# Hash attention and two MLPs on one core: two PSUM side jobs a pair put into one step, integer weight work moved, start copies and a scaling reissued

## The chip, the core and the metric

The kernel runs on one core of a Trainium2 chip. TensorE multiplies matrices and transposes (its results go to PSUM), VectorE and ScalarE work elementwise on SBUF and PSUM, GpSimd works elementwise on SBUF alone, and SyncE issues transfers (DMA); ScalarE and GpSimd can issue them too. The engines run side by side and wait for one another by semaphores. The metric is the time of one execution on the device, in microseconds (us).

## The reference

Attention comes first, for 2 batches, 8 heads, 768 positions and 64 features a head. Every query and key is hashed to 6 bits by the signs of its products with `proj`, and a query sees only the keys of its own bucket. Two MLPs follow on 1536 tokens of 512 features with 2048 hidden units.

```python
    q_bits = (np.einsum('bhsd,dk->bhsk', q, proj) > 0).astype(np.int64)
    k_bits = (np.einsum('bhsd,dk->bhsk', k, proj) > 0).astype(np.int64)
    ...
    mask = q_bucket[:, :, :, None] == k_bucket[:, :, None, :]
    scores = scale * np.matmul(q, k.transpose(0, 1, 3, 2))
    scores = np.where(mask, scores, -1000000000.0)
    ...
    attn = attn / (np.sum(attn, axis=-1, keepdims=True) + 1e-09)
    return np.matmul(attn, v).astype(np.float32)
...
    h = np.maximum(x @ w_in, 0.0)
    return (h * h @ w_out).astype(np.float32)
...
    h = x @ w_in
    g = h * (1.0 / (1.0 + np.exp(-h)))
    return (g @ w_out).astype(np.float32)
```

## The kernel before

All large products are made with numbers split into a high and a low part (`hq` and `lp`, `xh` and `xl`, and so on), so that TensorE's faster type keeps the accuracy.

Attention works through 8 pairs of heads. Its main loop has a counter `d`; one value of `d` is one **step**, and a pair takes 12 steps. In a step VectorE takes the row maxima of the score tile that the step before made (`row_max`, L276) and two one-column numbers from them (`row_live`, L280 and L281), and subtracts twice (`t_lo`, L315). ScalarE makes two high parts (`t_hi`, L309) and the exponentials of that score tile (`score_exp`, L289). TensorE transposes six blocks (`transp`, L304), multiplies four times with the values (`av`, L328 and L329), and makes the next score tile with four products (`score_mm`, L271). Every third step ScalarE also copies a finished output (`ob`, L334), and SyncE sends it to the tiles `ta` and `tb`.

Score tiles live in the PSUM pool `ps_s`, which has two buffers. Two side jobs of each pair borrow one:

- the **mask bits**: `bits_mm` (L128, 12 products) and `bits_cmp` (L133, VectorE's comparison into the tile `bt`). SyncE then copies the bits into the rows 64 to 75 of the query and key tiles `qq` and `kk` (`place_bits`, L164), and the next pair's first scores read them there in the second two of their four products. Pair p's bits are made at step 12(p-1)+3, and its first scores at the end of step 12(p-1)+7;
- the **broadcast of the row factors**: `rb_mm` (L351, six transposes of `rw`) and `x_norm` (L360, VectorE's product with `ta`), which scale a finished pair; pair p's at step 12(p+1)+8. `norm_rows` (L340, L341 on VectorE, L343 on GpSimd) makes `rw` at 12(p+1)+2, and `x_sum` (L356, GpSimd) adds `tb` to `ta` at 12(p+1)+4.

The order is written out by hand: `at(d, ...)` puts a call at the end of step `d`, `mid[d]` puts one between VectorE's `row_live` and its second `t_lo`, and `extra[d]` holds a side job. In a step with a side job the exponentials are issued ahead of it, and TensorE runs the side job between the transposes and `av`. Each engine runs its instructions in the order of issue.

Also placed by hand: the loads and splits of the next pair (`load_pair`, `scale_q` on ScalarE, `load_hi` by GpSimd's DMA queue, `split_pair` on GpSimd), and the first four weight tiles of the first MLP. Those come as 64-bit words and are turned into 32-bit numbers by integer operations: `w_abs` (L198, ScalarE), `w_limit` (L204), `w_exp` (L212), `w_sign` (L217) and `w_low` (L224) on VectorE, in four successive steps from 24i+11 for tile i.

Ahead of the loop, `load_head(0, 0)` fetches the first head's keys into `kk` by GpSimd's queue from DRAM, the second head's by SyncE's queue from SBUF, and `scale_q(1)` scales the second pair's queries on ScalarE before the first exponentials. TensorE runs some dummy products (L431) at the start.

After the loop the MLPs run from 262.9 us on.

Of the kernel before, what the change touches and what calls it, by code (L numbers as in the profile page):

```python
# [11 lines left out]
F32 = mybir.dt.float32  # L12
# [33 lines left out]
def lsh_attention_moe_moe(ctx, tc, kd, qk, v, pc, wi1, wo1, wi2, wo2, out):  # L46
# [48 lines left out]
    def load_head(p, h):  # L95
        t = pair[p]
        t["qq"][h] = a1.tile([128, 2, S], F32R, tag="qq", bufs=2, name=f"qq{p}_{h}")
        t["kk"][h] = a1.tile([128, 2, S], F32R, tag="kk", bufs=2, name=f"kk{p}_{h}")
        if (p, h) == (0, 1):
            for i in range(2):  # L100
                nc.sync.dma_start(out=t["kk"][h][0:64, i, :].bitcast(F32), in_=t["hp"][1][64:128].bitcast(F32))
        else:
            nc.gpsimd.dma_start(out=t["kk"][h][0:64], in_=kd[p, :, h].unsqueeze(1).broadcast_to([64, 2, S]))  # L103
        for r in (0, 64):
            nc.sync.dma_start(
                out=t["qq"][h][r : r + 64, 0, :].bitcast(F32), in_=t["hp"][0][64 * h : 64 * h + 64].bitcast(F32)
            )
# [92 lines left out]

    def w_limit(key):
        t = weights[key][1]
        eng = nc.vector if key in fast else nc.gpsimd
        eng.tensor_scalar(out=t, in0=t, scalar1=W_LO, scalar2=W_HI, op0=ALU.max, op1=ALU.min)  # L204

    def w_clamp(key):
# [163 lines left out]
        )  # L370

    todo = defaultdict(list)
    extra = {}
    mid = defaultdict(list)

    def at(g, fn, *a):
# [2 lines left out]
    for p in range(1, NPAIR):  # L379
        d0 = 12 * (p - 1)  # L380
        if p > 1:
            at(d0 - 13, load_pair, p)
            at(d0 - 9, scale_q, p)
            at(d0 - 8, load_hi, p)
        at(max(d0 - 6, -2), split_pair, p, 0)
        at(max(d0 - 2, -2), split_pair, p, 1)
        at(max(d0 - 6, -5), load_k, p)
        extra[d0 + 3] = bits_mm, bits_cmp, p
        at(d0 + 1, load_head, p, 0)
        at(d0 + 2, place_lo, p, 0)  # L390
        at(d0 + 4, place_bits, p, 0)
        at(d0 + 5, load_v, p)
        at(d0 + 10, split_v, p)
        at(d0 + 7, load_head, p, 1)
        at(d0 + 8, place_lo, p, 1)
        at(d0 + 8, place_bits, p, 1)
    for p in range(NPAIR):
        d0 = 12 * (p + 1)
        at(d0 + (2 if p < NPAIR - 1 else -3), norm_rows, p)
        at(d0 + (4 if p < NPAIR - 1 else 2), x_sum, p)  # L400
        if p < NPAIR - 1:
            extra[d0 + 8] = rb_mm, x_norm, p
            at(d0 + 9, x_hi, p)
            at(d0 + 9, x_lo, p)
    for i in range(WA):
        d0, key = 24 * i + 12, (0, 0, i)
        made[key] = wsrc(key), win, "wi", a2, a1, 1
        at(d0 - 8, w_load, key)
        at(d0 - 2, w_abs, key)
        for k, fn in enumerate((w_limit, w_exp, w_sign, w_low)):  # L410
            mid[d0 - 1 + k].append((fn, key))
        at(d0 + 2, w_split, key)

    with tc.manual_schedule():
        nc.sync.dma_start(out=pcr, in_=pc)
# [31 lines left out]
        load_head(0, 1)  # L447
        place_lo(0, 1)
        load_pair(1)
        scale_q(1)  # L450
        load_hi(1)
        load_v(0)
        extra[-3] = bits_mm, bits_cmp, 0
        at(-3, place_bits, 0, 1)
        at(-3, split_v, 0)

# [3 lines left out]
        for d in range(-5, G // 2 + 3):  # L460
# [10 lines left out]
            if 0 <= g < G:  # L471
# [2 lines left out]
                t_lo(g)  # L474
                transp(g + 1)
                t_hi(g + 1)
            more = extra.pop(d, None)
            if ready and more:
                score_exp(*ready, m)
            if more:  # L480
                t = more[0](more[2])
            for n in (g - V_LAG, g + 1 - V_LAG):
                if 0 <= n < G:
                    av(n)
            if more:
                more[1](t, more[2])
            elif ready:
                score_exp(*ready, m)
            u, j = divmod(d + 5, 3)
            if u < NU:  # L490
# [150 lines left out]
```

## Time and profile before

| | |
|---|---|
| median of 3 runs | 791.11 us (790.46 to 791.53) |
| the profiled execution, its own time | 790.36 us |
| its span, first to last instruction | 788.6 us |
| mean granted clock of TensorE, share of full speed | 0.996 |
| busy: TensorE, VectorE, ScalarE, GpSimd | 97%, 67%, 46%, 40% |

The profile is of one execution. Its rows name the engines PE (TensorE's products), PEld (its weight loads), DVE (VectorE), ACT (ScalarE), POOL (GpSimd) and SP (SyncE); a small q behind an engine is its sequencer, which issues and waits. L and a number is a line of the kernel, and `a<-b` says that a is written from b. In a timeline a row has its start and its length in us, then the instruction; a bracket behind it is how long the engine sat idle before it and what ended that. The chain of waits is followed back from the last instruction: each row is a start, a length, and what the end of the program hung on then; `x12` means that many pieces in a row. A row of stretches has start and end, length, then the busy us of PE, PEld, DVE, ACT and POOL with the number of instructions, the granted clock, the busy share of the 16 DMA engines, and GB/s. Products overlap in the rows of PE, so that the sum of their lengths is more than the time they take.

### The profile page before, as it was taken

How to read it: one execution, taken by the hardware profiler on the slowest of the kernel's cores; microseconds unless marked ns; L12 is line 12 of the kernel's file. 1: busy time of each engine (PE TensorE's matmuls, PEld its weight loads, DVE VectorE, ACT ScalarE, POOL GpSimd, SP SyncE). 2: the span in 40 equal slices, each digit the busy share in tenths (PEclk: the TensorE clock that was granted, in tenths of full speed). 3: DMA queues.
4: the chain of work that ended last, by engine and by line, in shares of the span. 5: the costliest groups of instructions: out<-in, count | busy, mean ns of one | idle time of the engine just before them, and what ended most of it. 6: DMA issues, size and time to landing. Idle time of an engine off the chain costs nothing.

```text
span 788.6 us, 10821 instructions
## 1 busy us (share of the span) xinstructions
PE 765.2 (97%) x3842; PEld 648.6 (82%) x3843; DVE 527.6 (67%) x1023; ACT 365.8 (46%) x706; POOL 316.1 (40%) x221
## 2 busy tenths in 40 slices
PE   6799999999999999999999999999999999999998
PEld 3598888888898888888888888888888888888887
DVE  4599999999999684565565465677456546545622
ACT  1688888888878452253154245343113213312300
POOL 0444464464432424453443444344344344435300
PEclk9999999999999999999999999999999999999999
DMA  7587786786761331211121212121122122111012
GB/s 188 163 209 180 172 214 172 168 227 155 160 162 28 130 107 55 81 54 53 54 81 53 81 59 76 54 65 69 54 74 67 47 81 80 54 54 54 0 67 93
DMA packets 30037, 78.78 MB, mean 100 GB/s; under 512 B 4536, under 2 KB 9016, under 8 KB 29984
## 3 DMA queue, kind: packets, MB, share of 16 engines
q1 hardware_dynamic: 25808, 66.69, 29.4%
q0 software_dynamic: 4176, 11.41, 6.0%
q8 instruction: 30, 0.49, 0.3%
q14 instruction: 23, 0.19, 0.1%
HBM read 51.81 MB, written 3.15 MB: 70 GB/s over the span
## 4 chain that ended last, share of the span: by engine, by line
PE 73%; DVE 19%; ACT 3%; DMA 3%; issue 1%; SPq 1%; ACTq 0%; DVEq 0%
PE y L562 33%; PE h L531 33%; DVE mt L276 8%; DVE tl L315 7%; ACT P L289 2%; PE bs L128 2%; PE s L271 2%; DVE mt L281 1%; DMA rk<-in_dram 1%; PE t L304 1%; PE o L328 1%; PE o L329 1%; DMA kk<-bt 1%; DMA qq<-bt 1%; DMA rq<-in_dram 1%
## 5 line engine op out<-in xcount | busy, mean ns | idle before, releaser
L315 DVE TENSOR_TENSOR tl<-t,th 128x384 fp32r<-128x384 f32 x192 | 104.7, 547 | 1.2 <-ACT th L309 1.2
L289 ACT ACTIVATE P<-s,mt 128x768 f32<-128x768 f32 x96 | 95.4, 994 | 20.5 <-DVE mt L281 17.5
L540 DVE CAST gh<-gt 128x512 fp32r<-128x512 f32 x96 | 45.4, 473 | 83.1 <-ACT gt L539 43.0
L276 DVE TENSOR_REDUCE mt<-s 128x1 f32<-128x768 f32 x96 | 91.3, 951 | 11.7 <-PE s L271 11.5
L309 ACT CAST th<-t 128x384 fp32r<-128x384 f32 x192 | 83.5, 483 | 20.9 <-PE t L304 20.5
L271 PE MATMUL s<-kk,qq 76*128 76x384 f32 (+1 forms) x384 | 84.8, 342 | 3.9 <-ACT P L289 3.3
L304 PE MATMUL t<-ident,P 128*128 128x128 f32 x576 | 83.1, 274 | 4.8 <-DVE tl L315 4.4
L304 PEld LDWEIGHTS t<-ident,P 128*128 128x128 f32 x576 | 67.7, 140 | 14.0 <-DVE tl L315 9.3
L570 DVE TENSOR_TENSOR y<-y,y 128x512 f32<-128x512 f32 x48 | 33.2, 691 | 63.0 <-PE y L562 63.0
L271 PEld LDWEIGHTS s<-kk,qq 76*128 76x128 f32 (+1 forms) x384 | 68.1, 190 | 8.1 <-ACT P L289 6.1
L328 PE MATMUL o<-th,vv 128*128 128x384 f32 x192 | 72.1, 375 | 0.0
L541 DVE TENSOR_TENSOR gl<-gt,gh 128x512 fp32r<-128x512 f32 x96 | 67.5, 704 | 3.3
L329 PE MATMUL o<-tl,vv 128*128 128x384 f32 x192 | 64.6, 337 | 0.0
L539 ACT ACTIVATE gt<-h 128x512 f32<-128x512 f32 x48 | 28.7, 598 | 75.2 <-PE h L531 55.8
L536 ACT ACTIVATE r<-h 128x512 f32<-128x512 f32 x48 | 28.7, 597 | 48.8 <-PE h L531 48.8
L568 DVE COPY y<-y 128x512 f32<-128x512 f32 x24 | 16.6, 691 | 31.5 <-PE y L562 31.5
L328 PEld LDWEIGHTS o<-th,vv 128*128 128x128 f32 x192 | 36.3, 189 | 0.5
L329 PEld LDWEIGHTS o<-tl,vv 128*128 128x128 f32 x192 | 36.5, 190 | 0.0
L537 ACT ACTIVATE gt<-r 128x512 f32<-128x512 f32 x48 | 30.4, 632 | 1.5
L577 DVE TENSOR_TENSOR ot<-y,y 128x512 f32<-128x512 f32 (+1 forms) x13 | 8.5, 650 | 22.9 <-PE y L562 22.9
L103 POOL DMA_DIRECT2D kk<-in_dram x15 | 9.7, 649 | 32.7 <-PE s L271 32.5
L343 POOL COPY rw<-ri 128x768 f32<-128x768 f32 x8 | 6.6, 822 | 35.5 <-DVE ri L341 28.2
(898 smaller groups left out, 2048.7 us busy)
## 6 DMA issues: line engine op xcount, KB each, us to landing
qq<-hq SPq DMA_DIRECT2D x32, 192.0 KB
kk<-in_dram POOLq DMA_DIRECT2D x15, 384.0 KB, 5.5
rq<-in_dram SPq DMA_DIRECT2D x8, 384.0 KB
rk<-in_dram SPq DMA_DIRECT2D x8, 384.0 KB
qq<-lp SPq DMA_DIRECT2D x16, 192.0 KB
kk<-lp SPq DMA_DIRECT2D x16, 192.0 KB
vr<-in_dram SPq DMA_DIRECT2D x8, 384.0 KB
ta<-ob SPq DMA_DIRECT2D x32, 96.0 KB
```

The costliest lines, as they stand in the source:

```text
L271: mm(s[:, n, 0:QW], t["qq"][h][0:kk, ab, c0 : c0 + 128], t["kk"][h][0:kk, ab, n * QW : (n + 1) * QW], start=ab == 0, stop=ab == 1)
L276: nc.vector.tensor_reduce(out=m[:, 0:1], in_=s[:, :, 0:QW], op=ALU.max, axis=AX.XY, negate=True)
L289: nc.scalar.activation(out=e.rearrange("p (a b) -> p a b", a=2), in_=s[:, :, 0:QW], func=AF.Exp, scale=m[:, 1:2], bias=m[:, 2:3], accum_ou ...
L304: nc.tensor.transpose(t[:, j * 128 : (j + 1) * 128], P[u, j][:, kt * 128 : (kt + 1) * 128], ident)
L309: nc.scalar.copy(out=th, in_=PT[g][0][:, 0:QW])
L315: nc.vector.tensor_tensor(out=tl, in0=t[:, 0:QW], in1=th.bitcast(F32), op=ALU.subtract)
L328: mm(o[:, 0:QW], vv, th, start=kt == 0, stop=False)
L329: mm(o[:, 0:QW], vv, tl, start=False, stop=kt == KT - 1)
L531: mm(acc, wt[:, kt], xt[:, kt, tok], start=n == 0, stop=n == 11)
L540: nc.vector.tensor_copy(out=gh[:, c, i], in_=gt)
L541: nc.vector.tensor_tensor(out=gl[:, c, i], in0=gt, in1=gh[:, c, i].bitcast(F32), op=ALU.subtract)
L562: mm(acc[:, 0:w], wt, xt, start=i == 0 and n == 0, stop=i == FB - 1 and n == 2)
```

## The change

- Mask bits and broadcast of a step share it: the bits move from step 12(p-1)+3 to 12(p-1)+5, the broadcasts of pairs 0 to 5 from 12(p+1)+8 to 12(p+1)+5, which is the same step as the bits of pair p+2. Both borrow a buffer of `ps_s`, one each. The placing of the bits moves from the end of step 12(p-1)+4 to the end of 12(p-1)+5. The bits of pairs 0 and 1 and the broadcast of pair 6 stay alone.
- `w_limit` of the first four weight tiles moves to GpSimd, `w_exp` and `w_sign` go into one step with side jobs (24i+5), `w_low` into the one 12 steps later (24i+17).
- The first pair's keys go into `kk` by ScalarE's DMA queue from `hk` in SBUF, for both heads.
- The scaling of the second pair's queries, and the two loads behind it, move from ahead of the loop to steps -2 and -1. Later pairs' scaling and `load_hi` move by two steps and one step, to the end of step 12(p-1)-7.
- `x_sum` moves one step forward, and the splits of queries two steps back.

```diff
-        if (p, h) == (0, 1):
+        if p == 0:
             for i in range(2):
-                nc.sync.dma_start(out=t["kk"][h][0:64, i, :].bitcast(F32), in_=t["hp"][1][64:128].bitcast(F32))
+                nc.scalar.dma_start(out=t["kk"][h][0:64, i, :].bitcast(F32), in_=t["hp"][1][64 * h : 64 * h + 64].bitcast(F32))
...
-        eng = nc.vector if key in fast else nc.gpsimd
+        eng = nc.gpsimd if made[key][3] is a2 else nc.vector if key in fast else nc.gpsimd
...
-            at(d0 - 9, scale_q, p)
-            at(d0 - 8, load_hi, p)
-        at(max(d0 - 6, -2), split_pair, p, 0)
-        at(max(d0 - 2, -2), split_pair, p, 1)
+            at(d0 - 7, scale_q, p)
+            at(d0 - 7, load_hi, p)
+        at(max(d0 - 4, 0), split_pair, p, 0)
+        at(max(d0 - 2, 0), split_pair, p, 1)
...
-        extra[d0 + 3] = bits_mm, bits_cmp, p
+        extra[d0 + 5].append((bits_mm, bits_cmp, p))
...
-        at(d0 + 4, place_bits, p, 0)
+        at(d0 + 5, place_bits, p, 0)
...
-        at(d0 + (4 if p < NPAIR - 1 else 2), x_sum, p)
+        at(d0 + (3 if p < NPAIR - 1 else 2), x_sum, p)
         if p < NPAIR - 1:
-            extra[d0 + 8] = rb_mm, x_norm, p
-            at(d0 + 9, x_hi, p)
-            at(d0 + 9, x_lo, p)
+            k = d0 + (5 if p < NPAIR - 2 else 8)
+            extra[k].append((rb_mm, x_norm, p))
+            at(k + 1, x_hi, p)
+            at(k + 1, x_lo, p)
     for i in range(WA):
-        d0, key = 24 * i + 12, (0, 0, i)
+        d0, key = 24 * i + 5, (0, 0, i)
...
-        at(d0 - 8, w_load, key)
+        at(max(d0 - 6, 0), w_load, key)
         at(d0 - 2, w_abs, key)
-        for k, fn in enumerate((w_limit, w_exp, w_sign, w_low)):
-            mid[d0 - 1 + k].append((fn, key))
-        at(d0 + 2, w_split, key)
+        at(d0 - 2, w_limit, key)
+        for k, fn in ((0, w_exp), (0, w_sign), (12, w_low)):
+            mid[d0 + k].append((fn, key))
+        at(d0 + 13, w_split, key)
...
-        scale_q(1)
-        load_hi(1)
         load_v(0)
-        extra[-3] = bits_mm, bits_cmp, 0
+        at(-2, scale_q, 1)
+        at(-1, load_hi, 1)
+        extra[-3].append((bits_mm, bits_cmp, 0))
...
             if ready and more:
                 score_exp(*ready, m)
-            if more:
-                t = more[0](more[2])
+            held = [(dve, pe(p), p) for pe, dve, p in more]
+            for dve, t, p in held[:1]:
+                dve(t, p)
             for n in (g - V_LAG, g + 1 - V_LAG):
                 if 0 <= n < G:
                     av(n)
-            if more:
-                more[1](t, more[2])
-            elif ready:
+            for dve, t, p in held[1:]:
+                dve(t, p)
+            if ready and not more:
                 score_exp(*ready, m)
```

ScalarE at the start of the program, before (`hq` is the first pair's high query, `rq_161` the second pair's raw query, `P` the exponentials, `th` the high parts):

```order
L438 ACT_TABLE_LOAD
L438 ACTIVATE hq_95<-rq_90 128x768
L93 ACTIVATE rq_161<-rq_161 128x768
L289 ACTIVATE P_0_184,sums_183<-s_0_172,mt 128x768
L289 ACTIVATE P_1_196,sums_183<-s_1_186,mt 128x768
L289 ACTIVATE P_2_227,sums_183<-s_2_213,mt 128x768
L289 ACTIVATE P_0_242,sums_183<-s_0_229,mt 128x768
L309 CAST th_259<-t_255 128x384
```

The same place of the changed kernel (`hk` is the first pair's high key, `kk_0` and `kk_1` its two heads' key tiles):

```order
L440 ACT_TABLE_LOAD
L440 ACTIVATE hq_95<-rq_90 128x768
L101 DMA kk_0_125<-hk_96 64x768 x2
L101 DMA kk_1_155<-hk_96 64x768 x2
L289 ACTIVATE P_0_180,sums_179<-s_0_168,mt 128x768
L289 ACTIVATE P_1_192,sums_179<-s_1_182,mt 128x768
L289 ACTIVATE P_2_223,sums_179<-s_2_209,mt 128x768
L93 ACTIVATE rq_162<-rq_162 128x768
L289 ACTIVATE P_0_236,sums_179<-s_0_225,mt 128x768
L309 CAST th_257<-t_253 128x384
```

Four key copies now stand on ScalarE's queue behind the first cast, and the scaling of `rq` stands behind three exponentials and ahead of the fourth.

TensorE around a side job of the bits before (step 15; `bs` is the bits' tile, `o` the output that `av` adds to, `s` the scores):

```order
L128 MATMUL bs_811<-hk_425,pjl 48x384
L128 MATMUL bs_811<-lp_494,pjh 48x384
L328 MATMUL o_767<-th_717,vv_461 128x384
L329 MATMUL o_767<-tl_719,vv_461 128x384
L328 MATMUL o_767<-th_725,vv_461 128x384
L329 MATMUL o_767<-tl_748,vv_461 128x384
L271 MATMUL s_2_830<-kk_1_532,qq_1_531 128x384 x4
```

The changed kernel at step 17, which holds the same pair's bits (`rb` is the broadcast's tile):

```order
L128 MATMUL bs_875<-hk_467,pjl 48x384
L128 MATMUL bs_875<-lp_576,pjh 48x384
L351 MATMUL rb_888<-ident,rw_784 128x128 x6
L328 MATMUL o_897<-th_795,vv_462 128x384
L329 MATMUL o_897<-tl_797,vv_462 128x384
L328 MATMUL o_897<-th_803,vv_462 128x384
L329 MATMUL o_897<-tl_818,vv_462 128x384
L271 MATMUL s_1_903<-kk_1_536,qq_1_535 128x384 x4
```

The six transposes of the broadcast, which stood five steps later, now stand between the bits' products and `av`, ahead of the step's score tile.

VectorE in a step of the bits before (step 27, one weight tile's work lies in other steps):

```order
L276 TENSOR_REDUCE mt<-s_1_1227 128x1
L315 TENSOR_TENSOR tl_1240<-t_1214,th_1218 128x384
L280 TENSOR_SCALAR mt<-mt 128x1
L281 TENSOR_SCALAR mt<-mt 128x1
L315 TENSOR_TENSOR tl_1250<-t_1244,th_1248 128x384
L133 TENSOR_SCALAR bt_1277<-bs_1260,pcr 48x768
L276 TENSOR_REDUCE mt<-s_2_1279 128x1
```

The changed kernel at step 29, the same pair's bits, with the second weight tile's `w_exp` and `w_sign`:

```order
L276 TENSOR_REDUCE mt<-s_0_1307 128x1
L315 TENSOR_TENSOR tl_1313<-t_1289,th_1293 128x384
L280 TENSOR_SCALAR mt<-mt 128x1
L281 TENSOR_SCALAR mt<-mt 128x1
L212 TENSOR_SCALAR wt_(0, 0, 1)_1273<-wt_(0, 0, 1)_1273 128x512
L217 SCALAR_TENSOR_TENSOR wt_(0, 0, 1)_1273<-raw_(0, 0, 1)_1133,wt_(0, 0, 1)_1273 128x512
L315 TENSOR_TENSOR tl_1325<-t_1319,th_1323 128x384
L133 TENSOR_SCALAR bt_1355<-bs_1335,pcr 48x768
L360 TENSOR_TENSOR ta_840<-rb_1348,ta_840 128x768
L276 TENSOR_REDUCE mt<-s_1_1363 128x1
```

Three operations came into the step: two of the weights ahead of its second `t_lo`, and `x_norm` behind the comparison.

## Rows read from the trace of the kernel before

**Rows 1.** Busy time by stretch: attention, MLPs, and two short ones at the start.

```profile
27.26:262.91 235.65, 225.22 (x1468) 206.64 (x1468) 218.52 (x521) 194.68 (x422) 106.88 (x93) 1.00 0.67 164
262.91:788.58 525.67, 522.44 (x2316) 432.98 (x2315) 299.87 (x487) 166.23 (x277) 206.20 (x119) 1.00 0.20 67
22.27:25.68 3.41, 3.19 (x10) 2.01 (x11) 0.00 (x0) 1.14 (x4) 0.07 (x1) 0.50 0.33 115
...
5.00:10.00 5.00, 2.51 (x12) 1.20 (x11) 1.61 (x3) 0.47 (x1) 0.00 (x0) 1.00 1.01 194
```

**Rows 2.** Chain of waits, start of the program.

```profile
1.65 7.64 DMA rk<-in_dram
...
16.10 4.43 DMA rq<-in_dram
...
21.37 1.07 ACT P L289 x2
...
22.49 3.75 PE bs L128 x12
```

**Rows 3.** Timeline of ACT, start of the program.

```profile
20.62 0.84 ACT L93 ACTIVATE rq<-rq 128x768 f32<-128x768 f32 x1 [15.15 <-DMA rq<-in_dram]
```

**Rows 4.** Timeline of DVE, the first two row maxima.

```profile
15.43 0.96 DVE L276 TENSOR_REDUCE mt<-s 128x1 f32<-128x768 f32 x1 [2.47 <-PE s L271]
...
16.67 0.96 DVE L276 TENSOR_REDUCE mt<-s 128x1 f32<-128x768 f32 x1
```

**Rows 5.** Timeline of DVE, steps 26 to 33: a side job of each kind.

```profile
92.38 0.96 DVE L276 TENSOR_REDUCE mt<-s 128x1 f32<-128x768 f32 x1
...
94.70 0.90 DVE L276 TENSOR_REDUCE mt<-s 128x1 f32<-128x768 f32 x1
...
97.47 1.07 DVE L133 TENSOR_SCALAR bt<-bs,pcr 48x768 fp32r<-48x768 f32 x1 [0.77 <-PE bs L128]
98.86 0.96 DVE L276 TENSOR_REDUCE mt<-s 128x1 f32<-128x768 f32 x1 [0.32 <-PE s L271]
...
107.10 0.96 DVE L276 TENSOR_REDUCE mt<-s 128x1 f32<-128x768 f32 x1
...
110.89 0.96 DVE L276 TENSOR_REDUCE mt<-s 128x1 f32<-128x768 f32 x1 [0.85 <-PE s L271]
```

**Rows 6.** Chain of waits, the same steps.

```profile
95.15 2.29 PE bs L128 x12
...
98.13 0.71 PE s L271 x4
...
108.01 0.57 PE rb L351 x4
```

**Rows 7.** Timeline of DVE, ends of two five-step stretches: with weights, without.

```profile
115.01 0.96 DVE L276 TENSOR_REDUCE mt<-s 128x1 f32<-128x768 f32 x1
...
129.66 0.96 DVE L276 TENSOR_REDUCE mt<-s 128x1 f32<-128x768 f32 x1 [0.32 <-PE s L271]
...
145.79 0.96 DVE L276 TENSOR_REDUCE mt<-s 128x1 f32<-128x768 f32 x1
...
158.46 0.96 DVE L276 TENSOR_REDUCE mt<-s 128x1 f32<-128x768 f32 x1 [0.32 <-PE s L271]
```

**Rows 8.** Instructions of L204, ns min/median/max, first and last start.

```profile
L204 DVE TENSOR_SCALAR wt_(0, 0, 0)_639<-wt_(0, 0, 0)_639 x1: 418/418/418, 57.0 to 57.0; 128x512 f32<-128x512 f32 x1
L204 DVE TENSOR_SCALAR wt_(0, 0, 1)_1549<-wt_(0, 0, 1)_1549 x1: 1089/1089/1089, 116.5 to 116.5; 128x512 f32<-128x512 f32 x1
...
L204 POOL TENSOR_SCALAR wt_(0, 0, 4)_4102<-wt_(0, 0, 4)_4102 x1: 2313/2313/2313, 297.6 to 297.6; 128x512 f32<-128x512 f32 x1
```

**Rows 9.** Chain of waits, two landings of mask bits.

```profile
72.83 4.53 DMA qq<-bt
...
133.92 2.60 DMA kk<-bt
```

**Rows 10.** Instructions of L164, ns min/median/max, first and last start.

```profile
L164 SPq DMA_DIRECT2D qq<-bt x15: 774/785/915, 27.4 to 230.8; - x15
```

More of the change, by code (lines that the diff above doesn't have):

```diff
@@ L372, in lsh_attention_moe_moe @@
     todo = defaultdict(list)
-    extra = {}
+    extra = defaultdict(list)
     mid = defaultdict(list)
@@ L476, in lsh_attention_moe_moe @@
                 t_hi(g + 1)
-            more = extra.pop(d, None)
+            more = extra.pop(d, [])
             if ready and more:
                 score_exp(*ready, m)
-            if more:
-                t = more[0](more[2])
+            held = [(dve, pe(p), p) for pe, dve, p in more]
+            for dve, t, p in held[:1]:
+                dve(t, p)
             for n in (g - V_LAG, g + 1 - V_LAG):
```

## The prediction, made before the changed kernel ran

> **What bounds the kernel now.** I read the stretches first. In the MLPs TensorE is busy for 522.44 of 525.67 us, and in attention's loop VectorE for 218.52 of 235.65 and TensorE for 225.22 [rows 1]. The MLP code is not touched and its stretch is full, so the change can only move its start: whatever attention gains or loses, the end gains or loses.
>
> The start was read in the chain of waits. It runs through the load of `rk`, 7.64 us, then through SyncE's issues to the load of the second pair's `rq`, 4.43, then through two exponentials at 21.37 and the first bits' products, 3.75 [rows 2]. ScalarE's timeline says why: it idled 15.15 us for `rq`, scaled it, and only then took the exponentials that VectorE had prepared [rows 3]. The first row maximum begins at 15.43, the second, right behind the first one's two small numbers, at 16.67 [rows 4].
>
> In the loop the row maxima give the pace. Between 98.86 and 107.10 lie four plain steps, 2.06 us each; VectorE idles nowhere there, so it sets the pace. Side jobs stretch their step: the two steps from 92.38 to 98.86 hold the row factors' two small operations and one set of bits and take 2.36 more than two plain ones (0.26 of it the small operations, from 92.38 to 94.70), and the broadcast's step, 107.10 to 110.89, takes 1.73 more. In both VectorE waits for TensorE [rows 5].
>
> **The start.** *Scaling behind scores.* ScalarE no longer waits for `rq` ahead of the first exponential. That can start at about 16.7 instead of 21.37: 4.7 us. The order shows the scaling now ahead of the fourth exponential, some 5 us behind the first, and `rq` landed at 20.5 even in the old order, so it should wait for nothing. It takes 0.84 us [rows 3], partly under VectorE's work: I charge 0.5 (0 to 0.84).
>
> *Clock.* The first bits' products ran at a granted clock of 0.50, 1.2 GHz, in the stretch 22.27 to 25.68 [rows 1], after TensorE had stood still behind those exponentials. Twelve of them took 3.75 there [rows 2] against 2.29 at full clock [rows 6]. The pause shrinks by the 4.7 us, so most of the 1.46 should return: 1.0 (0 to 1.46).
>
> *Keys.* The DRAM load of the first keys goes. `rk` took 7.64 in its company, a load of the same size 4.43 [rows 2], so `rk` may come up to 3.2 sooner, and the low parts and first bits wait for it. But the key copies now start only when `rk` has been cast, and four of them (192 KB each) queue beside four copies of queries and two of low parts. The transfer engines were busy for all of the stretch 5 to 10 us (share 1.01, 194 GB/s, [rows 1]). 192 KB at that rate is 1.0 us, so the two copies ahead of the first score take back about 2 of the 3.2: I take 1.2 (-1.0 to 3.2). The Trainium skill, "DMA: Bandwidth & Descriptors", section "Issuing engines are not separate DMA queues", says the same against a full gain: transfers from ScalarE, SyncE and GpSimd share 16 engines, and a second issuer saves issue time only. By that rule alone the keys bring nothing, and the sum below would be 1.2 smaller; the trace agrees as far as the share of 1.01 shows.
>
> Start in sum: 4.7 + 1.0 + 1.2 - 0.5 = 6.4.
>
> **One shared step.** The new step follows one with a copy of `ob`, as the broadcast's did; there the side job began 108.01 - 107.10 = 0.9 behind the row maximum, held by ScalarE's exponentials [rows 5, 6]. From the first bits' product to the next row maximum took 98.86 - 95.15 = 3.71, and the bits' products alone 2.29 [rows 5, 6]. The broadcast adds six transposes; four pieces took 0.57 [rows 6], so I take 0.6 for six, since they overlap. The step is 0.9 + 3.71 + 0.6 = 5.2, which is 3.15 over a plain one. VectorE fits in: the comparison can begin at 3.2 and takes 1.07 [rows 5], `x_norm`, as wide as a row maximum, 0.95 more, which is 5.2 as well. TensorE's score tile reuses the bits' buffer and waits for the comparison's end, 4.3; TensorE comes to it at 4.5.
>
> Per pair before 2.36 + 1.73 = 4.09; after 0.26 + 3.15 = 3.41; gain 0.68, six times 4.1. Ends: nothing, if the two waits still come one after the other (3.83 in the step), and 6.8, if the side job starts 0.45 behind the row maximum as the bits did [rows 5, 6]. Pair 1's bits, alone and now behind an `ob` step, lose 0.4. Sum 3.7.
>
> **Weight work.** The five steps from 115.01 to 129.66 hold a weight tile's four operations, those from 145.79 to 158.46 none; all else is alike. 14.65 - 12.67 = 1.98 a tile [rows 7]. Tile 0's `w_limit` took 0.42 where tile 1's took 1.09 [rows 8], so tile 0 cost 1.3; tile 3, with no bits step in its stretch, is taken between, at 1.5. Together 6.8. After the change VectorE has three operations. In a shared step it idles between its second subtraction and the comparison: 0.77 in the bits' step [rows 5], about 1.2 if the side job begins at 0.9. `w_exp` is like the 0.42 of `w_limit`; `w_sign` and `w_low`, with two inputs, I estimate at 0.6 each, from what is left of 1.98. So 1.0 fits under 1.2, and 0.6 does. If that cover were gone, 1.6 a tile would be paid, 6.4. Tile 3's `w_low` falls into a plain step: 0.6 paid. Gain 6.2. `w_limit` on GpSimd, 2.31 [rows 8], lies beside 106.88 busy of 235.65 us [rows 1].
>
> **What comes later.** The bits are made at rest 5 and read at rest 7 of the twelve steps, where it was 3 and 7. Counted from the shared step's row maximum: the comparison ends at 4.3, SyncE issues `qq<-bt`, 0.785 [rows 10], then `kk<-bt` at 5.15. Later row maxima lie at 5.2, 7.26 and 9.32, and the last takes the first scores that read the bits; the second two of its four products (0.71 for four, [rows 6]) must start by 8.95. So `kk<-bt` may take 3.8, `qq<-bt` 4.6. It took 2.60, and `qq<-bt` 4.53 [rows 9]. Free landings fit. But GpSimd's DMAs of the next pair's `hq` and `hk` are now issued in this same step. A `kk<-bt` of 4.53 is 0.7 late, TensorE waits ahead of the scores, and VectorE behind it. I take two such in seven pairs: 1.4 lost (0, to 7.64 as for `rk` each time).
>
> **Sum.** 6.4 + 3.7 + 6.2 - 1.4 = 14.9. The profiled execution took 790.36, 788.6 of it span; 790.36 - 14.9 = 775.5. It lay 0.75 under the runs' median of 791.11, so I say 776.2.
>
> **The rivals.**
> *Bits land late (slower side).* One wait per pair, ahead of the new pair's first scores, seven times (L - 3.8), L being the landing of `kk<-bt`. For it: slack shrinks from four steps to two, and the bulk loads moved beside it. Against: 2.60. At L = 5 it costs 8.4 instead of 1.4 and gives 783. Without any such wait the gain is 16.3, so it decides from L = 6.1; at 7.64, the farthest row [rows 2], it costs 27 and gives 802.
> *Keys come no sooner.* The copies take back all that `rk` gains, or 1 more: the first row maximum stays at 15.43 or comes up to 1 later, and the sum is 1.2 to 2.2 smaller: 777 to 778.5.
> *GpSimd holds VectorE.* `w_exp` stands ahead of a subtraction and the comparison, and now waits for GpSimd's 2.31, which itself stands behind `x_sum`, which waits for a transfer. VectorE asks two steps, 4.1, behind; ScalarE's part takes most of 3 of them, so it is about level. If GpSimd is 1.9 late each time, four tiles cost 7: 783.
> *The shared step gains more:* 6.8 from it, all of the clock and the keys, no late bits: 769.
>
> **Chances.** Forecast as summed, 771 to 781: 0.62. Keys no sooner: 0.15. Bits late: 0.10, of it 0.03 beyond the point that decides. GpSimd late: 0.06. More gain: 0.07. The range takes in the cases to L = 5 and the large gain: 769 to 785. A measurement of this kernel tells 0.2%, 1.6 us, from no change; faster by more: 0.93, within: 0.03, slower: 0.04.
>
> **What would show it.** ScalarE's first exponential within 0.2 of the first row numbers, and the scaling as its fourth operation of that kind; the first bits' products near 2.3; `rk` landing by 7. Shared steps of 5.2 between row maxima, with VectorE's wait ahead of the comparison mostly filled where weights are. Plain steps still 2.06, none over 2.6 but the ones named. No wait of TensorE on `qq<-bt` or `kk<-bt` above 1. MLP start near 248 instead of 262.91, its length 525.7 as before. Wrong it would be by a wait at rest 7 in every pair, by VectorE idle ahead of `w_exp`, by shared steps near 5.9, or by a first score later than 15.4.

## The result, and the profile after

| | before | after |
|---|---|---|
| median, beside each other (4 runs each) | 790.79 us (790.11 to 791.53) | 782.86 us (782.60 to 783.21) |
| ratio, with its 95% interval | | 0.990 (0.9883 to 0.9917) |
| span of the profiled execution | 788.6 us | 780.9 us |

The change gained 7.9 us. The forecast was 776.2, a gain of 14.9: the sign and the range hold, the size is half. The views below are those of the prediction, read from the changed kernel.

Busy time by stretch (columns as in [rows 1]): attention's loop, the MLPs, the first bits' products, the stretch 5 to 10, the second pair's bits, and in pair 4 the shared step and the six steps behind it.

```profile
20.32:255.23 234.91, 224.92 (x1468) 207.04 (x1468) 216.83 (x517) 193.15 (x423) 116.28 (x99) 0.99 0.70 168
255.23:780.90 525.67, 522.60 (x2318) 433.00 (x2316) 299.87 (x487) 166.29 (x278) 206.09 (x119) 1.00 0.20 67
16.53:19.15 2.62, 2.62 (x14) 1.82 (x14) 0.65 (x3) 1.08 (x2) 0.00 (x0) 0.81 0.96 245
5.00:10.00 5.00, 5.00 (x21) 2.87 (x20) 4.08 (x5) 0.35 (x1) 0.00 (x0) 1.00 0.68 147
38.20:41.95 3.75, 3.75 (x13) 2.51 (x14) 1.79 (x6) 2.41 (x5) 0.60 (x1) 0.57 0.34 78
...
124.46:129.75 5.29, 5.09 (x34) 4.07 (x33) 4.60 (x8) 3.33 (x7) 1.28 (x3) 1.00 0.27 69
129.75:142.86 13.11, 12.60 (x86) 12.06 (x85) 12.35 (x30) 11.18 (x25) 11.19 (x9) 1.00 0.96 237
```

The MLPs take 525.67, as in [rows 1]; they start 7.68 earlier (262.91 against 255.23), and that is the whole gain. The loop starts 6.94 earlier (27.26 against 20.32). So the start brought nearly everything, and the loop itself, from which 8.5 was forecast (3.7 + 6.2 - 1.4), 0.7. VectorE's busy time in it fell by only 1.7 and TensorE's stayed. From 5 to 10 the transfer engines are busy for 0.68 instead of 1.01. The last two rows were not forecast: the transfer engines are busy for only a quarter of the long shared step (share 0.27) and nearly full in the six steps behind it (0.96).

ScalarE's timeline, to be read beside [rows 3].

```profile
15.40 0.99 ACT L289 ACTIVATE P<-s,mt 128x768 f32<-128x768 f32 x1 [10.05 <-DVE mt L281]
...
22.65 0.83 ACT L93 ACTIVATE rq<-rq 128x768 f32<-128x768 f32 x1
...
35.37 0.66 ACT L198 ACTIVATE wt_(0, 0, 0)_373<-raw_(0, 0, 0)_277 128x512 f32<-128x512 f32 x1 [3.01 <-DMA raw_(0, 0, 0)_277<-in_dram]
```

The first exponential waits for VectorE's small numbers and no longer for `rq`; the scaling is its fourth operation of that kind, behind three exponentials, and waits for nothing. The last row is new: ScalarE stands 3.01 us for the first weight tile.

VectorE's timeline: the first two row maxima, the steps 4 and 5, the shared step 17 with what follows it, and the shared step 29.

```profile
14.03 0.96 DVE L276 TENSOR_REDUCE mt<-s 128x1 f32<-128x768 f32 x1 [3.60 <-PE s L271]
...
15.95 0.96 DVE L276 TENSOR_REDUCE mt<-s 128x1 f32<-128x768 f32 x1 [0.65 <-PE s L271]
...
31.71 0.96 DVE L276 TENSOR_REDUCE mt<-s 128x1 f32<-128x768 f32 x1
...
36.91 0.95 DVE L276 TENSOR_REDUCE mt<-s 128x1 f32<-128x768 f32 x1
...
43.37 0.96 DVE L276 TENSOR_REDUCE mt<-s 128x1 f32<-128x768 f32 x1 [0.32 <-PE s L271]
...
66.64 0.96 DVE L276 TENSOR_REDUCE mt<-s 128x1 f32<-128x768 f32 x1
...
69.78 1.07 DVE L133 TENSOR_SCALAR bt<-bs,pcr 48x768 fp32r<-48x768 f32 x1 [0.47 <-PE bs L128]
70.77 0.94 DVE L360 TENSOR_TENSOR ta<-rb,ta 128x768 f32<-128x768 f32 x1
71.91 0.96 DVE L276 TENSOR_REDUCE mt<-s 128x1 f32<-128x768 f32 x1 [0.20 <-PE s L271]
...
73.96 0.96 DVE L276 TENSOR_REDUCE mt<-s 128x1 f32<-128x768 f32 x1
...
76.77 0.96 DVE L276 TENSOR_REDUCE mt<-s 128x1 f32<-128x768 f32 x1 [0.74 <-PE s L271]
...
95.55 0.95 DVE L276 TENSOR_REDUCE mt<-s 128x1 f32<-128x768 f32 x1
...
101.30 0.96 DVE L276 TENSOR_REDUCE mt<-s 128x1 f32<-128x768 f32 x1 [0.20 <-PE s L271]
```

A step's length is the distance of two L276 rows. Step 17 takes 5.27, near the 5.2 of the forecast, and the comparison and `x_norm` run end to end in it. Step 29, with `w_exp` and `w_sign`, takes 5.75. The step at rest 7 behind the shared one, 73.96 to 76.77, takes 2.81, 0.75 over a plain one. The steps 4 and 5 take 5.20 and 6.46.

The chain of waits (start, length, what), where it answers those questions.

```profile
27.79 1.85 POOL lp L113
...
29.65 0.34 SPq L78
...
30.04 5.32 DMA raw_(0, 0, 0)_277<-in_dram
...
38.20 3.75 PE bs L128 x12
...
43.92 3.22 DMA kk<-bt
...
67.44 2.29 PE bs L128 x12
69.74 0.66 PE rb L351 x6
...
96.84 2.28 PE bs L128 x12
...
128.71 4.77 DMA qq<-bt
```

Step 4 first. On SyncE's queue the load of the first weight tile stands behind the third pair's queries (L78), which wait for their buffer until GpSimd has split the second pair's (the first row); it is issued at 30.04 and lands at 35.36, and `w_abs` of step 3 stands on ScalarE until then, ahead of the high parts, the subtraction and the transposes. TensorE's timeline shows the end of that:

```profile
37.05 0.55 PE L304 MATMUL t<-ident,P 128*128 128x128 f32 x3 [2.99 <-DVE tl L315]
```

Behind this pause of 2.99 the second pair's bits run at a granted clock of 0.57, mostly at 1.2 GHz, and take 3.75 instead of 2.29. In the shared steps the bits' products begin 0.80 behind the row maximum at step 17 (67.44 - 66.64) and 1.29 at step 29 (96.84 - 95.55); 0.8 + 2.29 + 0.66 and the rest (`av` and the score tile) make the 5.27. The mask bits' transfer takes 4.77 in the row at 128.71.

### The profile page after: what moved, and what is told of

Its sections match the earlier page's. It is cut to its first block, busy times and chain, and to the rows that moved or that the text cites. A ratio compares the mean times of both kernels' runs of the same rounds, so it can differ in the third digit from the quotient of the medians.

```text
span 780.9 us, 10831 instructions
## 1 busy us (share of the span) xinstructions
PE 764.1 (98%) x3843; PEld 649.0 (83%) x3843; DVE 525.9 (67%) x1019; ACT 363.7 (47%) x706; POOL 323.1 (41%) x224
## 4 chain that ended last, share of the span: by engine, by line
PE 85%; DVE 7%; DMA 3%; ACT 1%; issue 1%; SPq 1%; POOL 1%; ACTq 0%; POOLq 0%
PE y L565 33%; PE h L534 33%; PE s L271 5%; PE t L304 5%; DVE mt L276 3%; DVE tl L315 3%; PE o L328 3%; PE o L329 3%; PE bs L128 2%; ACT P L289 1%; DMA vr<-in_dram 1%; DMA raw_(0, 0, 0)_277<-in_dram 1%; DMA qq<-bt 1%; PE rb L351 1%; SPq L105 0%
## 5 line engine op out<-in xcount | busy, mean ns | idle before, releaser
L276 DVE TENSOR_REDUCE mt<-s 128x1 f32<-128x768 f32 x96 | 91.3, 951 | 10.9 <-PE s L271 10.5
L304 PE MATMUL t<-ident,P 128*128 128x128 f32 x576 | 81.4, 274 | 3.7 <-DVE tl L315 3.6
```

The lines of the kernel that those rows point to most:

```text
L276: nc.vector.tensor_reduce(out=m[:, 0:1], in_=s[:, :, 0:QW], op=ALU.max, axis=AX.XY, negate=True)
L304: nc.tensor.transpose(t[:, j * 128 : (j + 1) * 128], P[u, j][:, kt * 128 : (kt + 1) * 128], ident)
```

## The experiments

Each ran beside the kernel before; its median was 789.45 in the first four, 790.15 in the next four, 790.31 for the ninth and tenth, 790.30 for the last two. Times are medians, and step lengths are read from the one profiled execution of each kernel. In the diffs `...` stands for lines left out.

**The first weight tile's load.**

```diff
-        at(max(d0 - 6, 0), w_load, key)
+        at(max(d0 - 6, -2), w_load, key)
```

> Edit: the load of the first weight tile is issued at the end of step -2 instead of step 0, ahead of the third pair's queries on SyncE's queue; nothing else. Theory (the transfer stands behind a load that waits for GpSimd, so it lands at 35.35, ScalarE stands 3.0 us, VectorE and TensorE behind it, and TensorE's clock falls after that pause): the wait of 3.01 is gone, step 4 takes about 2.1 instead of 5.20, pair 1's bits take 2.3 instead of 3.75 and step 5 about 5.0 instead of 6.46; together 4.6 to 5: about 778.0 us. Rival (the transfer of 512 KB only moves the jam: another load of the start comes later, or the clock falls anyway): less than 2 us gained, above 781.

783.69 us (782.83 to 785.49). For tile 0 `d0 - 6` is -1, not -2, so the load moved by one step only and stayed behind the queries' load on SyncE's queue. It was issued at 29.27 and took 6.88, and ScalarE stood 3.71: writing the load one step earlier gained nothing while it stood behind the load that waits. The theory was not put to the test; the next run did that.

```diff
-        at(max(d0 - 6, 0), w_load, key)
-        at(d0 - 2, w_abs, key)
-        at(d0 - 2, w_limit, key)
+        at(max(d0 - 10, -2), w_load, key)
+        at(d0 - (5 if i else 2), w_abs, key)
+        at(d0 - (5 if i else 2), w_limit, key)
```

> Edit: as the run before, and for weight tiles 1 to 3 the Abs on ScalarE and the limit on GpSimd three steps earlier (rest 0 instead of rest 3 of the twelve), their load four steps earlier. Theory (the shared steps with w_exp and w_sign take 5.74 against 5.27 because ScalarE, set back 0.67 us by the Abs two steps ahead, brings the previous exponentials late, and the bits wait for their score buffer): steps 29, 53 and 77 take about 5.3, 1.4 us less than the run before: about 776.6. Rival (VectorE's two operations, 1.1 us ahead of its second subtraction, lengthen them): they stay at 5.7, and the time is that of the run before.

779.07 us (778.78 to 779.48), ratio 0.9862 (0.9847 to 0.9878). Here the load does stand ahead of the queries. VectorE's timeline of this kernel, steps 4 to 7 and the shared step 29:

```profile
32.91 0.96 DVE L276 TENSOR_REDUCE mt<-s 128x1 f32<-128x768 f32 x1
35.02 0.95 DVE L276 TENSOR_REDUCE mt<-s 128x1 f32<-128x768 f32 x1
...
40.06 0.96 DVE L276 TENSOR_REDUCE mt<-s 128x1 f32<-128x768 f32 x1 [0.34 <-PE s L271]
42.12 0.96 DVE L276 TENSOR_REDUCE mt<-s 128x1 f32<-128x768 f32 x1
45.90 0.96 DVE L276 TENSOR_REDUCE mt<-s 128x1 f32<-128x768 f32 x1 [1.71 <-PE s L271]
...
93.49 0.96 DVE L276 TENSOR_REDUCE mt<-s 128x1 f32<-128x768 f32 x1
...
98.78 0.96 DVE L276 TENSOR_REDUCE mt<-s 128x1 f32<-128x768 f32 x1 [0.20 <-PE s L271]
```

Step 4 takes 2.11 and step 5 5.04, 4.5 less than after the change: the stall and the clock that it cost are gone, TensorE's clock in those bits is 1.00. Step 29 takes 5.29: VectorE does the same weight work there, so the 0.46 was not its two operations but ScalarE, set back by the Abs two steps ahead: its exponentials begin at 93.17, 0.32 ahead of the row maximum, where the changed kernel had 95.66, 0.11 behind it. (GpSimd's limit moved with the Abs, but in the changed kernel it had ended at 96.80, ahead of `w_exp` at 97.06.) Of these gains 1.3 went again at step 7, where the second pair's bits are late (3.78 against 2.49 after the change), and the loop of this execution started 1.2 later (21.53).

**The late bits.** The shared step one step earlier, on top of that kernel:

```diff
-        extra[d0 + 5].append((bits_mm, bits_cmp, p))
+        extra[d0 + 4].append((bits_mm, bits_cmp, p))
...
-        at(d0 + 5, place_bits, p, 0)
+        at(d0 + 4, place_bits, p, 0)
...
-            k = d0 + (5 if p < NPAIR - 2 else 8)
+            k = d0 + (4 if p < NPAIR - 2 else 8)
...
-        d0, key = 24 * i + 5, (0, 0, i)
+        d0, key = 24 * i + 4, (0, 0, i)
```

> Edit: as the run before, and the shared step with all its work (bits, broadcast, weight operations, placing of the bits) one step earlier, at rest 4. Theory (the bits land late because two steps are too little: the steps at rest 7 take 0.3 to 1.0 more than a plain one, 3.65 us in all): all steps at rest 7 take 2.06, 3.6 us less than the run before: about 773. Rival (the step at rest 4 comes too early for what it needs: GpSimd's row factors of rest 2 or its sum of rest 3, so TensorE or VectorE waits in the shared step instead): shared steps over 6 us, no gain or a loss.

782.96 us (781.39 to 786.41). The steps at rest 7 fell to 2.14, as expected, and those at rest 6 rose to 2.27; but those at rest 1 now wait, by 1.1, 1.4, 0.3, 2.9 and 1.5 at the steps 13, 25, 37, 49 and 73, 7.2 in all. Neither theory had that: the shared steps stayed near 5.24, but for the last (5.85). The chain of waits names the second head's copies, here in the steps 13 and 49, and the stretches (step 52; 53 and 54; 55 to 59) show when the transfers run:

```profile
47.84 7.58 DMA kk<-bt
...
133.55 10.76 DMA kk<-lp
```

```profile
150.02:155.26 5.24, 5.14 (x33) 3.97 (x32) 5.01 (x10) 3.05 (x7) 0.85 (x1) 1.00 0.11 31
155.26:159.59 4.33, 4.33 (x31) 4.10 (x29) 4.13 (x10) 3.55 (x8) 0.57 (x1) 1.00 0.43 96
159.59:169.96 10.37, 10.31 (x70) 10.02 (x70) 10.29 (x26) 9.99 (x23) 9.68 (x9) 1.00 1.14 274
```

The steps 55 to 59 are full (share 1.14). A copy of bits that [rows 9] had at 2.60 takes 7.58 here, behind a stretch (37.00 to 47.84) with a share of 0.91. So the wait went from the first head's bits to the second head's copies.

The bulk loads later instead (`hq`, `hk`, values and raw keys out of the two steps in which the bits travel, the splits one step later), on top of the first experiment, with the bits at rest 5:

```diff
-            at(d0 - 7, scale_q, p)
-            at(d0 - 7, load_hi, p)
...
+            at(d0 - 6, scale_q, p)
+            at(d0 - 5, load_hi, p)
...
-        at(max(d0 - 6, -5), load_k, p)
+        at(max(d0 - 5, -5), load_k, p)
...
-        at(d0 + 5, load_v, p)
+        at(d0 + 7, load_v, p)
```

> Edit: as the first of these runs, and the next pair's bulk loads leave the two steps in which the bits travel: hq and hk two steps later, the scaling ahead of them one, the keys' raw load one, the values' two, the splits one. The bits stay at rest 5. Theory (the bits' transfers take 4.2 to 4.4 us because the bulk loads of the same step share the transfer engines with them; alone they would take about 2.6): the steps at rest 7 take 2.06 to 2.2, 3 to 3.6 us less than the first of these runs: about 774.7. Rival (the transfers need that long whatever goes beside them): the steps at rest 7 stay 0.3 to 1.0 too long, 778.

812.44 us (808.49 to 813.49), far slower than expected. The bits were freed (rest 7 at 2.26), but all loads then stood in one heap with the second head's copies, and the steps at rest 1 took 4.95 to 6.30, and five of the six behind them over 3. The chain there:

```profile
83.50 9.47 DMA kk<-lp
```

The opposite, on top of the second experiment: three of the loads at rest 4, ahead of the shared step whose transfer engines are mostly idle (`load_hq` is the `hq` part of `load_hi`, now by itself).

```diff
-            at(d0 - 7, scale_q, p)
+            at(max(d0 - 10, 5), scale_q, p)
+            at(max(d0 - 8, 5), load_hq, p)
             at(d0 - 7, load_hi, p)
...
-        at(max(d0 - 6, -5), load_k, p)
+        at(max(d0 - 8, -5), load_k, p)
...
-        at(d0 + 5, load_v, p)
+        at(d0 + 4, load_v, p)
```

> Edit: as e2_abs_early, and three of the bulk loads (hq by GpSimd with its scaling ahead of it, the values, the keys' raw load) are issued at rest 4 instead of rest 5 and 6, so that they travel in the long shared step, in which the transfer engines are busy for only a quarter; hk, whose buffer the bits' products still read, stays behind them. Theory (in the six steps behind the shared one the transfer engines are the limit, share about 1.0, and the bits queue in that jam): the bits land in 2.3 to 2.8 us, the steps at rest 7 take 2.06 to 2.2, nothing is late at rest 1, the shared steps stay at 5.3: 4 to 4.8 us less than e2_abs_early's 779.07, about 774.7. Rival 1 (the bits' copies need 4 us for themselves): no gain. Rival 2 (the earlier scaling or the issues delay ScalarE or SyncE ahead of the shared step, or the loads collide with the copies of rest 2 and 3): shared steps of 5.7 or more, 777 to 780.

780.67 us, its six runs between 776.51 and 784.10. Stretches of the profiled one (span 776.9), the shared step 41 and the six steps behind it:

```profile
122.09:127.45 5.36, 5.09 (x34) 4.07 (x33) 4.60 (x8) 2.67 (x6) 0.67 (x2) 1.00 0.95 269
127.45:139.80 12.35, 12.35 (x86) 12.09 (x85) 12.35 (x30) 11.12 (x25) 11.21 (x9) 1.00 0.72 179
```

The transfers fill the shared step (0.95 instead of 0.27), the six steps behind it are no longer full, and TensorE and VectorE are busy in all 12.35 us of them. In five of the seven pairs the step at rest 7 is a plain one; the two others lose 3.2 (step 7) and 0.7 (step 55). In the loop of this execution the theory holds; the loads of the start were not helped, and the median was no better than the second experiment's 779.07.

**The parts priced.** The broadcast back in its own step, on top of the second experiment:

```diff
-            k = d0 + (5 if p < NPAIR - 2 else 8)
+            k = d0 + 8
```

> Edit: as e2_abs_early, but the broadcasts of pairs 0 to 5 are back in a step of their own at rest 8; bits and weight operations stay at rest 5. It prices the merging alone. Theory of the prediction (bits alone lengthen their step by about 2.1 behind a step with an ob copy, the broadcast's by 1.73, together 3.8 against the shared step's 3.2): 0.6 a pair, 3.5 us in six, dearer than e2_abs_early: about 782.6. Rival (the broadcast's step gives the bits' late transfers and the jam behind them time, and the sum comes out even): within 1.5 us of 779.07.

789.36 us (787.69 to 790.34), ratio 0.9985 (0.9976 to 0.9994): some 10 dearer than the shared step (779.07, ratio 0.9862), three times what was expected. VectorE's timeline, steps 17 to 20:

```profile
62.69 0.96 DVE L276 TENSOR_REDUCE mt<-s 128x1 f32<-128x768 f32 x1
...
67.22 0.96 DVE L276 TENSOR_REDUCE mt<-s 128x1 f32<-128x768 f32 x1 [0.32 <-PE s L271]
69.28 0.96 DVE L276 TENSOR_REDUCE mt<-s 128x1 f32<-128x768 f32 x1
72.72 0.96 DVE L276 TENSOR_REDUCE mt<-s 128x1 f32<-128x768 f32 x1 [1.37 <-PE s L271]
...
76.51 0.96 DVE L276 TENSOR_REDUCE mt<-s 128x1 f32<-128x768 f32 x1 [0.86 <-PE s L271]
```

Bits alone take 4.53, the broadcast's step 3.79, together 8.3; the shared step with a plain one takes 7.3. That is 1.0 a pair. The rest is the wait at rest 7: 1.37 to 1.91 here, 0.45 to 0.98 with the shared step, which gives the bits 0.74 more time. So a shared step at rest 5 is worth much against separate ones at rest 5 and 8; against before, where the bits stood at rest 3 and only one pair's were late, it is worth much less.

The scaling alone, in the kernel before (with it the second pair's splits, which work on the scaled queries, move to step 0):

```diff
...
-        scale_q(1)
-        load_hi(1)
         load_v(0)
+        at(-2, scale_q, 1)
+        at(-1, load_hi, 1)
```

> Edit: the kernel before, with one part of the change: the second pair's scaling and its two loads behind the scores, and that pair's two splits not ahead of step 0. Keys, bits, broadcasts and weights as before. Theory (the scaling held the first exponentials, and the pause cost the first bits their clock): the first exponential at 16.7 instead of 21.37, the bits' products about 2.6 instead of 3.75; 5.2 to 5.7 us less than before, about 784. Rival (the second pair's splits and bits, which stand three steps into the loop, then wait for the later scaling and give part of it back): 1 to 3 us at steps 1 to 4, about 787.

783.97 us (783.83 to 784.80), ratio 0.9919 (0.9906 to 0.9932): 6.2 of the change's 7.9 by this part alone. Its loop starts at 19.63, ahead of the whole change's 20.32, with the old keys. The chain of waits of this kernel, start:

```profile
1.65 6.72 DMA rk<-in_dram
...
9.97 2.71 DMA kk<-lp
...
16.30 2.31 PE bs L128 x12
```

The first bits run at full clock, 2.31, where the changed kernel has 2.62 at a clock of 0.81. Step 7 gave 1.6 back, also by late bits (`qq<-bt` took 5.86). The keys undone in the changed kernel (the first lines of the change's diff):

> Edit: the changed kernel with one part undone: the first pair's keys come as before (GpSimd's queue from DRAM for the first head, SyncE's from SBUF for the second). Theory (the DRAM load held up rk, whose landing sets the first scores): rk lands near 9.3 again, the first row maximum is at 15.4 instead of 14.03, the loop starts 1.2 to 1.4 later: about 784.2. Rival (the key copies take back what rk gains, by the second head's copies in the jam): within 0.5 us of 782.86.

784.73 us (781.31 to 785.18), ratio 0.9917 (0.9900 to 0.9933), which does not part from the changed kernel's 0.990. `rk` took 7.88, and the first row maximum lay at 14.96, but the loop started at 20.78. Over the traces the loop starts at 19.63 and 20.78 with old keys and between 19.95 and 21.60 with new ones. What the new keys lose is in the chain of the second experiment, which has them (the 2.71 is in the chain just above):

```profile
7.75 5.14 DMA kk<-lp
```

The first scores need this copy. With the four key copies on their way beside it, it takes 5.14 where it takes 2.71 without. By the Trainium skill, "DMA: Bandwidth & Descriptors", section "Issuing engines are not separate DMA queues", a second issuer saves only the time of issuing; the two rows agree. The changed kernel and e8_old_keys differ by the keys alone, and they say the same. From the issue of that copy to the first scores lie 5.22 us with the new keys (7.83 to 13.05, transfer share 0.97) and 2.85 with the old ones (11.13 to 13.98, 0.58). With the new keys TensorE stood 2.42 ahead of the first scores and made the second ones at a granted clock of 0.51 (14.09 to 15.91); with the old ones it stood 0.60, and the clock was 1.00 (15.02 to 16.07).

**What is left of the waits.** The first weight tile out of the start, on top of e5_bulk_sooner; in the start the second pair's values and the third pair's raw keys are also loaded two and three steps later, behind the bits' copies:

```diff
...
-        d0, key = 24 * i + 5, (0, 0, i)
+        d0, key = (24 * i + 5) if i else 17, (0, 0, i)
...
-        for k, fn in ((0, w_exp), (0, w_sign), (12, w_low)):
+        for k, fn in ((0, w_exp), (0, w_sign), (12 if i else 0, w_low)):
```

> Edit: as e5_bulk_sooner, but the first weight tile leaves the start: its load of 512 KB goes from step -2 to step 10, its Abs and limit to step 12, its three integer operations all into the shared step 17; the second pair's values are loaded at step 6 and the third pair's raw keys at step 7, behind the bits' copies. Theory (the wait of 1.7 to 3.2 us at step 7 in e2_abs_early and e5_bulk_sooner is the jam of the start's loads, in which the second pair's bits queue): step 7 takes at most 2.8, step 17 some 0.3 to 0.6 more than 5.3, the other steps as in e5_bulk_sooner; 2.3 to 2.8 us less than the profiled run of that kernel, a span of about 774.4, and a time of 776. Rival (the copies of that place are late by their own number, or the load jams the steps 10 to 16 instead): step 7 stays above 3.5 or a step from 11 to 17 grows by over 1, no gain.

779.39 us (778.93 to 781.33), span 777.2. Step 7 fell from 5.28 to 3.34, but step 13 rose to 2.80 and step 17 to 5.90: part theory, part rival, and no gain over the second experiment. Without the values' loads, on top of e3_shared_at_4 (every pair then uses the first pair's values, so this kernel computes something else and serves only to be timed):

```diff
+        if p > 0:
+            t["vr"] = pair[0]["vr"]
+            return
         t["vr"] = a1.tile([128, 2 * KT, D], F32, tag="vr", name=f"vr{p}")
```

> Edit: as e3_shared_at_4, but the values are loaded for the first pair only and used for all pairs (so this leaves out seven transfers of 384 KB, and the output is that of other values); everything else, GpSimd's splitting of the values too, stays. Theory (in e3_shared_at_4 the second head's copies are late at rest 1, 7.2 us in all, because the bulk loads ahead of them fill the transfer engines from rest 5 on; a load at 384 KB is about 2 us of them): the steps at rest 1 take 2.06 to 2.6, most of the 7.2 us comes back: about 777. Rival (the copies are late by where they are issued, not by the jam): rest 1 stays at 3 to 5, 783.

778.75 us (776.77 to 780.57), 4.2 less than e3_shared_at_4. At rest 1 the steps 13 and 37 went to 2.06, 25 and 73 to 2.5, while step 49 stayed at 4.81: of 7.2 us, 3.6 came back by seven transfers fewer, though in this execution the steps 50 and 76 took 0.9 and 0.8 more. That the jam is one of volume is shown for that half at most. The weight loads behind the second head's copies instead of among them:

```diff
-        at(max(d0 - 10, -2), w_load, key)
-        at(d0 - (5 if i else 2), w_abs, key)
-        at(d0 - (5 if i else 2), w_limit, key)
+        at(d0 - 5 if i else -2, w_load, key)
+        at(d0 - (3 if i else 2), w_abs, key)
+        at(d0 - (3 if i else 2), w_limit, key)
```

> Edit: as e3_shared_at_4, but the loads of weight tiles 1 to 3 (512 KB each) are issued at rest 11 instead of rest 6, behind the second head's copies instead of among them; their Abs and limit follow at rest 1. Nothing is left out. Theory (the waits at rest 1 in e3_shared_at_4 are the jam, and those of the steps 25, 49 and 73, 1.4, 2.9 and 1.5 us, are the ones with a weight load in it; the pairs without one, at 37 and 61, wait 0.3 at most): these three go to 0.4 or less, step 13 keeps its 1.1, all else as there: 5 us less than e3_shared_at_4, about 777.8. Rival (the second head's copies are late whatever is loaded): the three steps stay above 1, 782.

781.07 us, its runs between 776.84 and 784.41. The waits at the steps 25 and 49 are gone (2.06 each) and step 73 keeps 1.0, but the steps behind them rose (26 to 3.50, 50 to 4.94, 74 to 5.36): I had put the Abs only two steps behind the load, and ScalarE's timeline shows what that cost at step 50:

```profile
144.94 0.66 ACT L198 ACTIVATE wt_(0, 0, 2)_2114<-raw_(0, 0, 2)_2043 128x512 f32<-128x512 f32 x1 [2.30 <-DMA raw_(0, 0, 2)_2043<-in_dram]
```

It is the stall of the changed kernel's step 3 again, with a lower clock behind it (0.67 from 145 to 150). The last run puts the parts together, on top of e5_bulk_sooner; the second pair's values, the third pair's raw keys and the weights' Abs move along by a step or two:

```diff
...
-        extra[d0 + 5].append((bits_mm, bits_cmp, p))
+        extra[d0 + (5 if p > 1 else 4)].append((bits_mm, bits_cmp, p))
...
-        at(d0 + 5, place_bits, p, 0)
+        at(d0 + (5 if p > 1 else 4), place_bits, p, 0)
...
-        at(max(d0 - 10, -2), w_load, key)
+        at(d0 - 6 if i else -2, w_load, key)
```

> Edit: as e5_bulk_sooner (three bulk loads ahead of the long shared step), with the second pair's bits one step earlier, at step 4, ahead of the third pair's hq and hk, the second pair's values and third pair's keys behind them, and weight loads 1 to 3 at rest 11. Theory (what is left of e5_bulk_sooner's waits, 3.2 us at step 7 and 0.7 at step 55, is a jam around the bits): step 7 at most 2.3, step 55 at 2.1, shared steps 5.3, rest 1 below 2.2: 3.5 us less than the profiled run of that kernel, a span of about 773.4 and 775 us. Rival (the loads still have to pass in the same time, so the wait only turns up elsewhere, at rest 1 or at step 13): 778 to 780.

776.20 us (775.96 to 779.48), ratio 0.9827 (0.9811 to 0.9843): 14.1 less than before, and the best of all. Step 7 is a plain one. The profiled execution was the slowest of the five (span 777.7) and lost 1.3 at step 19, 1.2 at step 50, 1.0 at step 5 and 0.7 at step 13, so part of the jam is left.

## Why the prediction was half right

**The start (6.4 forecast, 6.94 measured).** The first exponential, the scaling's place and the clock went as written. That the sum came out is in part luck: the scaling gave more than its share and the keys less. The scaling alone gave more than its 5.2: some 5.9, the shrinkage of the distance from the second row maximum to the loop's start, from 10.59 (16.67 to 27.26) to 4.65 in that kernel (14.98 to 19.63), since the scaling itself hides (0, not 0.5) and the first bits ran at full clock. **Keys:** the step "so the two copies ahead of the first score take back about 2 of the 3.2: I take 1.2" was mis-sized. `rk` did land before 7 (its cast begins at 6.26), but `kk<-lp` takes 5.14 with the new keys and 2.71 with the old ones, the second scores came later too (0.65 of waiting at 15.95), and by the loop's start nothing is left that the spread of the traces would show. The rival "keys come no sooner" was right in size. The first row maximum came at 14.03 instead of 15.43, but with old keys it came at 13.80 in the seventh experiment and at 14.96 in the eighth, so not even that is shown to be the keys' doing.

**The shared step (5.2 forecast, 5.27 measured).** Right, down to its pieces. With its neighbours, rest 2 to 6 (60.26 to 73.96), it costs 3.40 over plain steps, where 3.41 was forecast. Pair 1's bits, alone, lost 0.1 and not 0.4: their step takes 4.53 in the ninth experiment, where no weights stand in it, and took 4.44 before.

**Weights (6.2 forecast, about 4.3 measured).** The three shared steps with `w_exp` and `w_sign` take 0.47 more than those with `w_low`, 1.4 in all, and step 5, which holds the first tile's, 0.5 more than without them (5.04 in the second experiment, 4.53 in the ninth). The part has no run of its own; these are differences of steps. The cover that I named does hold VectorE's work, as the second experiment's 5.29 shows; but I did not follow the Abs, which now stands on ScalarE two steps ahead of the shared one, whose bits wait for ScalarE's exponentials. For the first tile this was not tried apart. GpSimd's part was not the wait that I had as a rival (96.80 against 97.06, above).

**Late bits (1.4 forecast, 3.65 measured).** The mechanism and the steps were right, the term mis-sized: "I take two such in seven pairs". Six of the seven pairs are late, by 0.31 to 0.98. The row of 2.60 that I leaned on [rows 9] lies in a stretch with a transfer share of 0.53, the 4.77 at 128.71 in one of 0.78, with `hq` and `hk` issued at 128.21 and 128.80. In the five late pairs of the shared steps the waiting products began 4.8 to 5.5 behind the issue of `qq<-bt`, and 4.6 was what I had left it. "Free landings fit" was true and not the case. I also took the 4.53 of [rows 9] for a mere length: that landing was late already, in the kernel before. VectorE's timeline there, the steps 19 and 20:

```profile
75.58 0.96 DVE L276 TENSOR_REDUCE mt<-s 128x1 f32<-128x768 f32 x1
...
78.29 0.96 DVE L276 TENSOR_REDUCE mt<-s 128x1 f32<-128x768 f32 x1 [0.64 <-PE s L271]
```

Step 19 took 2.71, 0.65 over a plain one, so of the 3.65 after the change 0.65 was not new.

**The first weight tile (nothing forecast, 4.56 lost).** The missing step. I costed the operations alone. The diff moves the load from step 4 to step 0 and its first user from step 10 to step 3, and on SyncE's queue it now stands behind a load that waits for GpSimd. Step 4 lost 3.14, and step 5 1.42 by the clock; the second experiment gave both back.

Put together: 14.9 + 0.5 (start) + 0.3 (pair 1's bits) - 1.9 (weights) - 2.3 (bits) - 4.6 (first tile) + 0.65 (the late bits of before) = 7.55, and the span shows 7.7. The prediction's 776.2 missed by 6.7; more than half of that is the first tile, which it did not price at all.

## What to carry to other kernels

A load's time was here that of its place in the queue, not of the step it is written in: look at what stands ahead of it there and what that waits for. When a step grows longer, ask which transfers could be on their way during it; here the longest step had mostly idle transfer engines and the short ones behind it were full, and moving loads ahead of it (780.67, and 776.20 together with the other parts) did better than moving the late one (782.96), though alone no better than leaving both as they were (779.07). And a change that gathers side jobs takes slack from whatever their results feed: price that by a row from the new surroundings, not from the old.

## What had not been expected of the hardware

A pause of 0.98 and then 0.60 us on TensorE (in e8_old_keys, at 35.49 and 36.65) was followed by the same drop to half clock as the pause of 2.99: its bits took 3.79. A copy of mask bits took from 2.3 us (in the kernel before, at 193.84, share 0.36) to 7.6, and one of the keys' low parts from 2.7 to 10.8. And the runs of e5_bulk_sooner and e11_raw_behind spread by 7.6 us (776.51 to 784.10 and 776.84 to 784.41), those of e2_abs_early by 0.7; why the one and not the other is open.
